# Attention outputs of two parity blocks transposed by one DMA, pad copies made for two blocks at once, and a new order of all jobs

## Chip, cores and metric

The kernel runs on one core of one Trainium2 chip. The metric is the device time of one execution in microseconds. The core has five engines with instruction queues of their own: TensorE (PE in the profile; PEld are its weight loads), VectorE (DVE), ScalarE (ACT), GpSimd (POOL) and SyncE (SP), which here only issues DMAs.

## The reference

One layer: an attention block, then a gated block with a product over the sequence, both behind a layer norm and with a residual.

```python
def _A_ref(x, wqkv, wo):                     # S = 2048, D = 448, H = 16 heads of 28
    W, dil = (8, 2)
    ...                                       # q, k, v = x @ wqkv
    off = jnp.arange(W) * dil                 # each position sees itself and 7 others, every second one back
    idx = pos[:, None] - off[None, :]
    ...
    attn = _softmax(logits, axis=-1)          # over the 8 positions, those before 0 masked out
    o = jnp.einsum('bhsw,bhswd->bhsd', attn, vg)
    return ... @ wo

def _B_ref(x, w_in, w_sp, b_sp, w_out):       # F = 1792, Fh = 896
    z = _gelu(jnp.einsum('bsd,df->bsf', x, w_in))
    z1 = z[..., :Fh]
    z2 = _layernorm(z[..., Fh:], axis=-1)
    g = jnp.einsum('ts,bsf->btf', w_sp, z2) + b_sp[None, :, None]
    return jnp.einsum('bsf,fd->bsd', z1 * g, w_out)

h = x + _A_ref(_layernorm(x), A_wqkv, A_wo)
out = h + _B_ref(_layernorm(h), B_w_in, B_w_sp, B_b_sp, B_w_out)
```

## The kernel before

All data stays on the chip in bf16; PSUM holds products in f32. The kernel is written as some 900 **jobs**, each a few instructions of one engine with the resources that they read and write. The constant `ORDER` (L33) is a list of job numbers: it is the order in which all jobs are issued to their engines' queues, found by a search ahead of time. Within an engine the list's order is the program's order; across engines, waits on semaphores follow from the resources. `BANKS` gives each use of PSUM its banks (of eight), `MODE` the way in which a product is split, `ON` the engine of a copy that several engines could make. Number 885 in `ORDER` (861 after the change) is a **warm** job: one matmul on constant data, put in where the plan has nothing for TensorE.

The names of jobs, with the tokens in 16 tiles `m` of 128:

- `x` loads, `st0`, `mv0`, `rs0`, `n0` (statistics, their sum, the root on POOL, the norm on VectorE) give a normalized tile in the ring `xn`. It has 448 columns and is padded to 512: copy `nd0` repeats its last 64 columns (L633), so that the fourth chunk of 64 inner rows lies on both halves of the partitions.
- `xT` turns a tile into columns: tiles 0 to 3 by TensorE with copies `xe`, tiles 4 to 15 by a transposing DMA on SP's queue.
- `qk2` to `qk5` (tiles of 256 or 512 tokens; `qk0`, `qk1` of 128) and `v` are the products with `wqkv`, copied out of PSUM by `qe` and `ve`.
- Attention runs in 17 **blocks** `b`. Blocks 0 to 15 come in pairs: an even one takes the even tokens of a stretch of 256, an odd one the odd ones; block 16 takes the rest. Per block: logits `lg` (two PSUM tickets, 28 inner rows each, four row groups at once), exponentials `ex` (ACT), mask `mk` (VectorE), output `o` (TensorE), `rc` and `om` (division, VectorE) into the ring `otm` of four slots, pad copy `od`, transposing DMA `oT` into `OTs`, and **column copy** `oc` from `OTs` into every second column of `OT` (L862), in two parts where the ring `OT` wraps (`oc8b`, `oc9b`).
- `y` projects two tiles with `wo` as soon as `OT` has their tokens (`COVER`), `h` adds the residual, `st1`, `mv1`, `rs1`, `n1`, pad copy `nd1` and transposing DMA `hT` (two tiles at once, L783) give the operand of the second block.
- `z2_m` and `z1_u` are the products with `w_in`, with `z2c`, `z2g`, `z1g` on ACT; `st2` to `n2` the second norm.
- `g` is the product with `w_sp`, `ua` and `um` the gate, `wo0` to `wo10` and `wp` the last product, `r` and `out` the result. `wlo` and `whi` are transposing loads of `w_sp`, `w_in0_0` and so on its weights.

A product of 448 inner rows has three full chunks and one of 64 rows. `MODE` 'FH' does the six full matmuls first and the two short ones, which run side by side on two row groups, second; 'HF' the other way; 'AB' cuts all into halves of 64 rows that run side by side, eight matmuls in part a and six in part b.

TensorE's order before, around the places that matter (part a and b of a product are two jobs):

```
... xT3 xT2 warm lg0_0 lg0_1 qk2_3a qk2_3b qk2_0a qk2_2a qk2_0b qk2_2b qk2_1a v2a qk2_1b v2b v0a lg2_0 lg1_0 v0b lg3_1 v4a v4b lg2_1 lg3_0 qk3_1a ...
... lg12_1 y4a lg12_0 lg13_1 y4b lg15_0 lg13_0 lg15_1 z2_1a o12 o10 v16a v16b lg16_0 z2_1b z2_2a ...
... y10a z1_0a y10b z1_0b z1_3a z1_6a z1_4a ...
```

SP's: `... x12 xT4 xT7 xT5 xT6 xT9 xT13 xT8 w_in0_1 xT10 xT11 xT12 xT14 oT0 oT1 xT15 w_in0_0 oT2 oT3 wlo5 ...`

Of the kernel before, what the change touches and what calls it, by code (L numbers as in the profile page):

```python
# [21 lines left out]
MODE = {'qk2_0': 'AB', 'qk2_1': 'AB', 'qk2_2': 'AB', 'qk2_3': 'FH', 'qk3_0': 'AB', 'qk3_1': 'AB', 'qk3_2': 'AB',  # L22
         'qk3_3': 'AB', 'qk4_0': 'AB', 'qk4_1': 'AB', 'qk4_2': 'AB', 'qk4_3': 'AB', 'qk5_0': 'AB', 'qk5_1': 'FH',
         'qk5_2': 'AB', 'qk5_3': 'FH', 'v0': 'AB', 'y0': 'AB', 'v2': 'AB', 'v4': 'FH', 'y2': 'AB', 'v6': 'AB', 'y4':
         'AB', 'v8': 'HF', 'y6': 'AB', 'v10': 'AB', 'y8': 'AB', 'v12': 'HF', 'y10': 'AB', 'v14': 'HF', 'y12': 'AB',
         'v16': 'FH', 'y14': 'AB', 'z2_0': 'AB', 'z2_1': 'AB', 'z2_2': 'AB', 'z2_3': 'HF', 'z2_4': 'AB', 'z2_5': 'AB',
         'z2_6': 'FH', 'z2_7': 'FH', 'z2_8': 'AB', 'z2_9': 'AB', 'z2_10': 'AB', 'z2_11': 'AB', 'z2_12': 'AB', 'z2_13':
         'AB', 'z2_14': 'AB', 'z2_15': 'AB', 'z1_0': 'AB', 'z1_1': 'AB', 'z1_2': 'FH', 'z1_3': 'HF', 'z1_4': 'FH',
         'z1_5': 'HF', 'z1_6': 'FH', 'z1_7': 'AB', 'z1_8': 'AB', 'z1_9': 'AB', 'z1_10': 'AB', 'z1_11': 'AB', 'z1_12':
         'AB', 'z1_13': 'AB', 'wo0': 'FF', 'wo2': 'FF', 'wo4': 'FF', 'wo6': 'FF', 'wo8': 'FF', 'wo10': 'FF'}  # L30
ORDER = [6, 26, 42, 27, 43, 29, 0, 885, 30, 885, 1, 31, 885, 885, 7, 885, 885, 28, 12, 885, 32, 885, 2, 52, 885, 134,
         885, 885, 5, 44, 33, 885, 885, 53, 3, 885, 34, 45, 54, 885, 135, 885, 4, 55, 46, 885, 885, 47, 16, 56, 885,
         885, 61, 35, 885, 9, 57, 48, 36, 885, 885, 59, 58, 885, 885, 11, 885, 37, 49, 62, 136, 885, 13, 885, 50, 145,  # L33
         38, 60, 51, 10, 63, 81, 146, 8, 137, 139, 82, 138, 39, 15, 140, 67, 64, 40, 17, 147, 83, 41, 148, 14, 84,
         141, 72, 85, 149, 70, 142, 150, 68, 73, 144, 71, 89, 65, 74, 69, 143, 885, 66, 94, 202, 75, 204, 160, 203,
         98, 76, 95, 161, 99, 77, 86, 205, 151, 90, 78, 87, 157, 96, 162, 152, 206, 158, 153, 154, 91, 159, 237, 79,
         97, 92, 155, 80, 113, 238, 156, 115, 199, 239, 114, 93, 88, 116, 117, 240, 100, 213, 119, 200, 241, 118, 253,
         120, 214, 201, 121, 262, 254, 104, 101, 105, 125, 263, 122, 242, 106, 264, 251, 110, 166, 123, 126, 102, 107,
         111, 252, 108, 127, 163, 243, 255, 167, 103, 164, 168, 256, 165, 207, 19, 257, 215, 244, 172, 109, 216, 258,
         169, 112, 217, 259, 173, 170, 208, 124, 174, 128, 209, 218, 129, 171, 245, 131, 219, 338, 132, 246, 339, 220,  # L40
         130, 247, 221, 210, 316, 248, 340, 178, 211, 317, 276, 305, 179, 222, 277, 181, 180, 306, 133, 212, 175, 265,
         18, 223, 278, 182, 266, 249, 176, 183, 279, 267, 260, 177, 280, 303, 184, 268, 224, 304, 697, 269, 185, 281,
         307, 186, 270, 21, 378, 250, 282, 693, 271, 283, 261, 314, 225, 272, 315, 698, 284, 379, 273, 226, 355, 380,
         300, 274, 318, 356, 341, 343, 301, 229, 344, 285, 227, 187, 342, 302, 190, 20, 228, 345, 692, 319, 308, 230,
         320, 275, 381, 321, 188, 23, 382, 231, 286, 22, 346, 309, 322, 189, 310, 191, 694, 287, 232, 192, 311, 347,
         233, 234, 392, 348, 288, 312, 235, 393, 193, 349, 289, 24, 353, 394, 194, 323, 354, 292, 290, 416, 417, 195,
         357, 395, 383, 293, 418, 196, 236, 384, 396, 313, 358, 324, 197, 350, 385, 454, 455, 198, 359, 25, 291, 360,
         397, 456, 294, 695, 421, 398, 325, 361, 399, 422, 352, 297, 419, 362, 295, 432, 351, 400, 326, 420, 296, 298,
         468, 327, 299, 433, 430, 423, 469, 470, 524, 471, 328, 424, 330, 431, 386, 699, 329, 425, 492, 387, 331, 426,
         493, 332, 495, 364, 388, 525, 363, 427, 494, 434, 534, 401, 526, 365, 472, 496, 535, 389, 366, 333, 536, 335,  # L50
         390, 334, 541, 457, 367, 336, 402, 542, 458, 337, 368, 435, 370, 543, 473, 436, 459, 371, 369, 497, 437, 372,
         460, 655, 474, 706, 475, 498, 438, 373, 476, 656, 461, 652, 544, 439, 499, 551, 653, 375, 374, 391, 657, 500,
         376, 545, 462, 428, 440, 654, 501, 552, 546, 403, 463, 553, 704, 547, 464, 558, 527, 465, 404, 377, 429, 502,
         554, 559, 528, 441, 537, 405, 649, 560, 466, 503, 538, 442, 529, 561, 650, 539, 707, 443, 658, 651, 667, 477,
         406, 444, 661, 446, 691, 445, 540, 696, 447, 408, 548, 659, 407, 555, 448, 504, 409, 549, 575, 660, 550, 556,
# [1079 lines left out]
```

## Time and profile before

| | us |
|---|---|
| median of 3 runs | 244.9 (244.74 to 245.12) |
| the profiled execution's own time | 247.0 |
| its span, first to last instruction | 245.3 |
| TensorE busy | 237.2 |
| VectorE busy | 147.6 |
| ACT busy | 91.1 |
| POOL busy | 42.5 |

The mean granted clock of TensorE was 0.993. In the profile a line like `L461` is a line of the kernel; L461 is the matmul of all products in `product`, L809 the logits, L833 the attention output, L987 and L1008 the product with `w_sp`, L1035 and L1056 the last one. `L504` is `move`, so every copy has that line and is told by its tiles. `psum<-wv,xhT` reads: writes psum, reads wv and xhT. "SPq" is a DMA's issue on SP's queue, "DMA a<-b" its transfer until it has landed. The timeline and the chain of waits give start, duration and instruction; in the timeline neighbours of one kind are merged ("x8").

### The profile page before, as it was taken

How to read it: one execution, taken by the hardware profiler on the slowest of the kernel's cores; microseconds unless marked ns; L12 is line 12 of the kernel's file. 1: busy time of each engine (PE TensorE's matmuls, PEld its weight loads, DVE VectorE, ACT ScalarE, POOL GpSimd, SP SyncE). 2: the span in 40 equal slices, each digit the busy share in tenths (PEclk: the TensorE clock that was granted, in tenths of full speed). 3: DMA queues.
4: the chain of work that ended last, by engine and by line, in shares of the span. 5: the costliest groups of instructions: out<-in, count | busy, mean ns of one | idle time of the engine just before them, and what ended most of it. 6: DMA issues, size and time to landing. Idle time of an engine off the chain costs nothing.

```text
span 245.3 us, 5632 instructions
## 1 busy us (share of the span) xinstructions
PE 237.2 (97%) x2422; PEld 122.3 (50%) x2422; DVE 147.6 (60%) x334; ACT 91.1 (37%) x109; POOL 42.5 (17%) x98
## 2 busy tenths in 40 slices
PE   7997999999999989999999999999999999999995
PEld 4763544554555534444555555555554444444453
DVE  5998685998999897899913030604217350060584
ACT  2485748968899956659711000000000000000000
POOL 6625022030533317052311000000000000000000
PEclk9997999999999999999999999999999999999999
DMA  6953527989688889957999700000000020000022
GB/s 175 294 157 70 129 61 110 189 174 186 128 107 112 88 146 225 253 59 134 166 178 181 141 3 0 3 0 3 0 3 0 0 92 24 0 3 0 3 90 97
DMA packets 66233, 23.20 MB, mean 95 GB/s; under 512 B 58656, under 2 KB 65952, under 8 KB 66208
## 3 DMA queue, kind: packets, MB, share of 16 engines
q1 hardware_dynamic: 66208, 22.83, 48.5%
q8 instruction: 19, 0.31, 0.5%
q14 instruction: 6, 0.05, 0.1%
HBM read 6.72 MB, written 1.84 MB: 35 GB/s over the span
## 4 chain that ended last, share of the span: by engine, by line
PE 80%; DMA 8%; DVE 7%; ACT 1%; SPq 1%; issue 1%; POOL 0%
PE psum L987 37%; PE psum L461 27%; PE psum L1035 7%; DMA hnT<-xn 4%; PE psum L1008 3%; PE psum L809 2%; PE psum L833 2%; PE psum L1056 2%; DMA wq<-in_A_wqkv_dram 2%; DVE st L620 2%; DMA xhT<-xn 2%; DVE E L824 1%; DVE xn L631 1%; DMA OTs<-otm 1%; DVE x_tm L774 1%; SPq L519 1%
## 5 line engine op out<-in xcount | busy, mean ns | idle before, releaser
L968 DVE TENSOR_TENSOR ub<-psum,bb 128x512 bf16<-128x512 f32 x28 | 18.1, 686 | 64.4 <-PE psum L987 64.4
L987 PE MATMUL psum<-wsp_hi,z2p 64*128 64x512 bf16 x384 | 42.2, 376 | 0.0
L818 ACT ACTIVATE E<-psum 128x960 bf16<-128x960 f32 (+2 forms) x34 | 31.5, 976 | 6.3 <-PE psum L809 6.3
L987 PEld LDWEIGHTS psum<-wsp_hi,z2p 64*128 64x128 bf16 x384 | 19.7, 94 | 21.9 <-DVE srg L1016 0.4
L987 PE MATMUL psum<-wsp_lb,z2p 64*128 64x512 bf16 x224 | 26.9, 376 | 0.0
L987 PE MATMUL psum<-wsp_la,z2p 64*128 64x512 bf16 x224 | 26.5, 376 | 0.0
L461 PE MATMUL psum<-w_in,hnT 64*128 64x448 bf16 (+1 forms) x206 | 24.6, 350 | 0.2 <-issue 0.2
L461 PE MATMUL psum<-hnT,w_in 64*128 64x512 bf16 (+1 forms) x166 | 23.7, 377 | 1.1 <-DMA hnT<-xn 0.9
L461 PE MATMUL psum<-xhT,wqk 64*128 64x512 bf16 (+3 forms) x206 | 24.4, 355 | 0.1
L898 DVE BATCH_NORM_STATS2 st<-z2p 128x6 f32<-128x448 bf16 x32 | 19.0, 610 | 8.0 <-ACT z2p L894 6.0
L824 DVE TENSOR_TENSOR E<-E,maskb 128x1920 bf16<-128x1920 bf16 (+2 forms) x17 | 19.8, 1183 | 2.9 <-ACT E L818 2.9
L620 DVE BATCH_NORM_STATS2 st<-x_tm 128x6 f32<-128x448 bf16 x32 | 18.8, 613 | 1.4 <-DMA x_tm<-in_A_x_dram 1.3
L987 PEld LDWEIGHTS psum<-wsp_lb,z2p 64*128 64x128 bf16 x224 | 12.8, 94 | 11.4
L987 PEld LDWEIGHTS psum<-wsp_la,z2p 64*128 64x128 bf16 x224 | 12.8, 94 | 11.4
L611 POOL TENSOR_TENSOR rs<-rs,negh 128x2 f32<-128x2 f32 (+2 forms) x23 | 17.4, 758 | 3.0 <-DVE rs L610 1.1
L936 ACT ACTIVATE z1p<-psum 128x1024 bf16<-128x1024 f32 x14 | 14.1, 1023 | 10.0 <-PE psum L461 10.0
L1035 PE MATMUL psum<-w_out,z1p 128*128 128x448 bf16 x84 | 16.4, 353 | 0.0
L461 PEld LDWEIGHTS psum<-w_in,hnT 64*128 64x128 bf16 (+1 forms) x206 | 10.9, 94 | 10.8 <-issue 1.0
L461 PE MATMUL psum<-wv,xhT 64*128 64x448 bf16 (+1 forms) x92 | 14.9, 367 | 1.4 <-DMA xhT<-xn 1.4
L504 ACT ACTIVATE qkT<-psum 128x1024 bf16<-128x1024 f32 (+1 forms) x17 | 13.3, 824 | 6.9 <-PE psum L461 4.2
L461 PEld LDWEIGHTS psum<-hnT,w_in 64*128 64x128 bf16 (+1 forms) x166 | 9.6, 95 | 12.4 <-DVE x_tm L774 1.4
L461 PEld LDWEIGHTS psum<-xhT,wqk 64*128 64x128 bf16 (+1 forms) x206 | 10.0, 95 | 9.8 <-issue 0.8
(68 smaller groups left out, 254.6 us busy)
## 6 DMA issues: line engine op xcount, KB each, us to landing
w_in<-in_B_w_in_dram SPq DMA_DIRECT2D x8, 224.0 KB, 3.7
out_dram<-srg SPq DMA_DIRECT2D x16, 112.0 KB, 1.7
x_tm<-in_A_x_dram SPq DMA_DIRECT2D x2, 448.0 KB, 5.2
w_out<-in_B_w_out_dram SPq DMA_DIRECT2D x1, 784.0 KB, 5.1
wq<-in_A_wqkv_dram SPq DMA_DIRECT2D x3, 224.0 KB, 4.5
x_tm<-in_A_x_dram SPq DMA_DIRECT2D x3, 224.0 KB, 3.4
bb<-in_B_b_sp_dram SPq DMA_DIRECT2D x1, 512.0 KB, 4.8
wv<-in_A_wqkv_dram SPq DMA_DIRECT2D x1, 336.0 KB, 4.8
```

Source lines behind the costliest of these rows:

```text
L461: ins = e.matmul(o, w, x, start=k not in seen, stop=last, **kw)
L504: j = pl.job(name, eng, key, [(lambda e: e.activation(o(), i(), AF.Copy) if eng == "act" else e.tensor_copy(o(), i()), list(reads), list(w ...
L611: power = (lambda e: e.tensor_tensor(R, A, negh[:, 0:1].to_broadcast([128, n]), ALU.pow), [rr, r_negh], r_rs[k][m:m + n])
L620: [(lambda e: e.bn_stats(st[:, m, :], src), [rsrc], [r_st[k][m]])], dve_t(D))
L818: return e.activation(o, i, AF.Exp, scale=SCALE)
L824: return e.tensor_tensor(a, a, maskb[:, mi:mi + 1, pad:pad + nq].to_broadcast([NK, NHEAD, nq]), ALU.mult)
L898: [(lambda e, m=m, k=k: e.bn_stats(st3[:, m, k, :], z2p[:, m, D * k:D * (k + 1)]), [r_z2[m]], [r_st[2][m]])], dve_t(D))
L936: return e.activation(o, i, AF.Gelu_apprx_tanh)
L968: [(lambda e: e.tensor_tensor(ub[:, s, :], psv(tk, k), bb[:, 512 * tc:512 * tc + 512], ALU.add), [r_bb], [r_ub[s]])], dve_t(512), use=[tk] ...
L987: ins = e.matmul(psv(tk, k), z2p[h, s, 128 * fc:128 * fc + 128], wsp(s, tc)[h], start=n == 0 and s == 0, stop=n == len(lots) - 1 and s == ...
L1008: ins = e.matmul(psv(tk), z2p[:, s, 128 * fc:128 * fc + 128], wsp(s, tc), start=(s == 0), stop=(s == NB - 1))
L1035: ins = e.matmul(psv(tk, k, D), z1p[h, fc, 128 * (m + k):128 * (m + k) + 128], w_out[h, fc, :], start=fc == 0 and (which == 0 or not half) ...
```

## The change

Three edits in the code, and new constants.

1. `project` no longer makes a pad copy `nd1` for each of two tiles; one copy, named `nd1_m` with the even m, does both, after the second norm.
2. For blocks 0 to 15 the pad copy `od` and the transposing DMA `oT` are made once for a pair, with the odd block's number: `od1`, `oT1`, `od3` and so on. The DMA takes two slots of `otm` (128 x 1024) into both halves of `OTs`. The column copies stay one per block and part; both blocks' copies follow the pair's DMA. Block 16 is as before.
3. `ORDER`, `BANKS`, `MODE` and `ON` are new. 24 jobs are gone.

```diff
             for i in range(2):
-                s = ln_norm(1, m + i, mv2, x_tm, r_h[m + i], kl, True)
+                s = ln_norm(1, m + i, mv2, x_tm, r_h[m + i], kl, False)
+            move("nd1_%d" % m, "pool", kl, lambda s=s: xn[:, s - 1:s + 1, D:512], lambda s=s: xn[:, s - 1:s + 1, 384:D], r_xn[s - 1:s + 1],
+                 r_xnd[s - 1:s + 1], {"pool": 0.5, "dve": 0.14})
...
-            move("od%d" % b, "pool", b + KEY["om"], lambda os=os, nq=nq: otm[0:nq, os, D:512], lambda os=os, nq=nq: otm[0:nq, os, 384:D],
-                 [r_otm[os]], [r_otd[os]], {"pool": 0.42, "dve": 0.1})
             t0 = k0 // step * step + step * pad
             if step == 1:
+                move("od%d" % b, "pool", b + KEY["om"], lambda os=os, nq=nq: otm[0:nq, os, D:512], lambda os=os, nq=nq: otm[0:nq, os, 384:D],
+                     [r_otm[os]], [r_otd[os]], {"pool": 0.42, "dve": 0.1})
                 dma_T("oT%d" % b, lambda o=t0 % OTR, n=nq: OT[:, :, o:o + n], lambda n=nq, os=os: otm[0:n, os, :],
                       [r_otm[os], r_otd[os]], [r_OT[t % OTR] for t in range(t0, t0 + nq)], b + KEY["oT"])
-            else:
-                dma_T("oT%d" % b, lambda b=b: OTs[:, b % 2], lambda os=os: otm[:, os, :], [r_otm[os], r_otd[os]], [r_OTs[b % 2]],
-                      b + KEY["oT"])
-                cut = min(nq, (OTR * (t0 // OTR + 1) - t0) // 2)
...
+            elif b % 2:
+                move("od%d" % b, "pool", b + KEY["om"], lambda os=os, nq=nq: otm[0:nq, os - 1:os + 1, D:512],
+                     lambda os=os, nq=nq: otm[0:nq, os - 1:os + 1, 384:D], r_otm[os - 1:os + 1], r_otd[os - 1:os + 1],
+                     {"pool": 0.5, "dve": 0.14})
+                load("oT%d" % b, lambda: OTs[:].rearrange("p m c t -> p (m c) t"), lambda os=os: otm[:, os - 1:os + 1, :],
+                     r_OTs, 1.3, (TLAT + 0.1, 1.0), key=b + KEY["oT"], transpose=True, reads=r_otm[os - 1:os + 1] + r_otd[os - 1:os + 1])
+                cut = min(nq, (OTR * (t0 // OTR + 1) - t0 // 2 * 2) // 2)
+                for par in range(2):
+                    for i, (a, z) in enumerate([(0, cut)] + ([(cut, nq)] if cut < nq else [])):
+                        o = (t0 + 2 * a) % OTR
+                        move("oc%d" % (b - 1 + par) + "b" * i, "pool", b + KEY["oT"],
...
```

What the constants come to, counted from the lists: warm jobs 29 before and 28 after. Engines of the copies that several can make: `ve` on VectorE four and two (`ve8` and `ve12` go to ACT); `oc` on POOL, ACT and VectorE 8, 7, 3 and 11, 4, 3; `nd` and `od` on POOL 24 and 16, on VectorE 21 and 13; weight copy `wp3` goes from VectorE to ACT; of the three `qe` on VectorE one is now `qe2_0`, of half the width. Jobs on SP: 113 and 105. Changes of TensorE's row grouping (full, halves, logits, transposes) from one job to the next: 73 before and 71 after, apart from those around the transposes on TensorE.

TensorE's order after, around the same places:

```
... qk0F2 xT2 xT3 qk0H qk1H warm warm qk2_2a qk2_3a qk2_3b qk2_2b lg0_0 lg0_1 qk2_0a qk2_1a qk2_0b qk2_1b v2a v0a lg3_0 lg2_0 v0b v2b v4a v4b lg3_1 o0 lg2_1 qk3_1a lg1_1 lg1_0 qk3_1b qk3_3a o3 o2 ...
... v14a lg10_1 qk5_3a qk5_3b v14b y4a lg12_0 lg15_1 y4b z2_1a z2_1b lg12_1 lg13_1 y6a lg13_0 y6b lg15_0 o10 o12 lg14_0 lg16_0 v16a v16b z2_2a ...
... z1_6b y10a z1_5b z2_5a y10b z1_3a z2_5b z1_3b z1_4a ...
```

SP's: `... x12 xT5 xT4 xT6 xT7 xT8 xT11 xT10 xT9 w_in0_0 w_in0_1 xT13 xT14 wlo5 oT1 xT12 xT15 oT3 wlo6 wlo1 ...`

VectorE's around the first transposes: `... n0_2 mv0_6 n0_3 mv0_5 st0_7 xe2_0 mv0_7 xe3_0 n0_5 st0_11 n0_4 mv0_11 st0_8 nd0_4 ...`, and around h4: `... mk9 mk11 h2 rc9 st1_2 rc11 om9 oc7 st1_3 om11 mk10 mv1_3 mv1_2 h4 n1_2 st1_4 st1_5 mv1_4 n1_3 mv1_5 mk12 h6 ...`

29 lines of the change are left out of this document (12 added, 17 removed), and 103 rows, old and new, of tables (BANKS, MODE, ORDER).

## The prediction

> **What bounds the kernel now.** I read the busy shares first, then the stages, then the waits of TensorE, then the timeline around them.
>
> ```profile
> PE 237.2 (97%) x2422; PEld 122.3 (50%) x2422; DVE 147.6 (60%) x334; ACT 91.1 (37%) x109; POOL 42.5 (17%) x98
> ```
>
> TensorE is busy 97% of the span. The matmuls to do stay the same, so the end moves only with the time in which TensorE waits or runs slowly. The stages tell where that is (from and to, length, then the busy time of PE, PEld, DVE, ACT and POOL with their instructions, the granted clock, the DMA share and GB/s):
>
> ```profile
> 0.00:20.00 20.00, 17.83 (x227) 12.53 (x229) 16.79 (x52) 10.88 (x18) 10.40 (x33) 1.00 0.71 200
> 20.00:21.70 1.70, 0.34 (x9) 0.20 (x8) 1.70 (x6) 1.70 (x3) 1.62 (x3) 1.00 0.47 71
> 21.70:25.40 3.70, 3.70 (x28) 1.35 (x30) 1.99 (x8) 1.24 (x3) 0.94 (x4) 0.54 0.37 75
> 25.40:66.20 40.80, 40.62 (x584) 20.32 (x580) 34.99 (x64) 30.80 (x36) 9.73 (x18) 1.00 0.74 137
> 66.20:68.10 1.90, 1.27 (x28) 0.74 (x28) 1.73 (x2) 1.90 (x3) 0.00 (x0) 1.00 0.83 179
> 68.10:88.40 20.30, 20.30 (x274) 10.81 (x274) 19.13 (x43) 19.05 (x24) 6.20 (x13) 1.00 0.85 108
> 88.40:89.50 1.10, 0.15 (x4) 0.08 (x2) 1.10 (x2) 0.95 (x1) 0.00 (x0) 1.00 0.97 97
> 89.50:123.60 34.10, 33.95 (x296) 16.49 (x298) 30.79 (x83) 22.61 (x26) 12.63 (x27) 1.00 0.91 168
> 123.60:245.30 121.70, 119.00 (x991) 59.77 (x985) 39.41 (x80) 1.94 (x2) 0.93 (x2) 1.00 0.19 40
> ```
>
> From 123.6 on, TensorE lacks only 2.7 us, which is the tail after the last matmul; a new order can gain nothing there. Before that it loses time in four places: the start, 20 to 25.4, 66.2 to 68.1 and 88.4 to 89.5. The last three have names:
>
> ```profile
> PE psum L461 <- DMA xhT<-xn: 1.4, 1, 1.4
> PE psum L461 <- DMA hnT<-xn: 0.9, 1, 0.9
> PE psum L809 <- DVE x_tm L774: 0.5, 1, 0.5
> ```
>
> ```profile
> 17.35 4.17 DMA xhT<-xn
> ```
>
> ```profile
> 57.22 0.42 PE L809 MATMUL psum<-qkT 28*128 28x120 bf16 x16
> 57.57 0.82 PE L461 MATMUL psum<-xhT,wqk 64*128 64x512 bf16 x6
> 58.23 1.59 PE L461 MATMUL psum<-wv,xhT 64*128 64x448 bf16 x8
> ```
>
> ```profile
> 21.66 2.62 PE L461 MATMUL psum<-wv,xhT 128*128 128x448 bf16 x8 [1.36 <-DMA xhT<-xn]
> ...
> 66.26 0.79 PE L809 MATMUL psum<-qkT 28*128 28x120 bf16 x16
> ...
> 67.52 0.39 PE L809 MATMUL psum<-qkT 28*128 28x120 bf16 x8 [0.47 <-DVE x_tm L774]
> ...
> 68.07 0.93 PE L461 MATMUL psum<-w_in,hnT 64*128 64x448 bf16 x8 [0.16 <-issue]
> ```
>
> The first is v4, which needs transpose xT5, third on SP's queue: issued at 17.35, landed 4.17 us later. TensorE stood still 1.36 us, and then the clock was near half (0.54) for 3.7 us. The eight matmuls of v4 took 2.62 us, those of v12 at full clock 1.59: 1.0 us, and some 0.2 us in the pieces behind it. The second is the logits around 66.3: 24 matmuls take 1.81 us to the next product (68.07 less 66.26), where 16 take 0.35 (57.57 less 57.22), so 24 want some 0.6; 1.2 us are lost, because h4 frees its PSUM bank late. The third is z1_3, which waited 0.9 us for transpose hT6. Together 1.4 + 1.2 + 1.2 + 0.9 = 4.7 us.
>
> **The change, part by part.** *Fewer transposes and copies.* Sixteen oT transposes become eight of double width, sixteen od copies eight, sixteen nd1 copies eight.
>
> ```profile
> L518 SPq DMA_TRANSPOSE OTs<-otm x16: 1190/1210/1676, 34.9 to 88.7; - x16
> L504 POOL COPY otm<-otm x9: 236/237/1257, 30.6 to 83.6; 120x64 bf16<-120x64 bf16 x8, 128x64 bf16<-128x64 bf16 x1
> L504 POOL COPY OT<-OTs x8: 617/744/1363, 37.4 to 93.2; 128x480 bf16<-128x480 bf16 x5, 128x512 bf16<-128x512 bf16 x2, 128x384 bf16<-128x384 bf16 x1
> ```
>
> ```profile
> L518 SPq DMA_TRANSPOSE hnT<-xn x8: 1231/1269/2364, 58.1 to 111.4; - x8
> ...
> DMA to landing us min/median/max: 3.1/3.8/5.2
> ```
>
> A transpose of double width already runs here, as hT: 1.27 us of SP's queue against 1.21 for one oT, so eight fewer free some 9 us of SP. POOL loses eight small copies net and takes eleven column copies (oc) where it had eight, 3 x 0.74 = 2.2 us more, roughly what the small ones free. None of this is TensorE's work: it lies beside it and is worth nothing until it makes an operand land earlier, which the next parts count. A copy of double width is not in the trace; I take 0.4 us on POOL, between 0.24 (one copy) and 0.48 (two), and it enters one chain below.
>
> ```profile
> 34.91 2.51 SPq L518 DMA_TRANSPOSE OTs<-otm  x2
> ```
>
> Pairing makes the even block wait for the odd one. Before, blocks 0 and 1 were transposed from 34.91, one behind the other. After, o1 comes some 1.5 us sooner, the one paired transpose goes out at about 33.5, lands by 36.5 (hT's median of 3.8 us less one for a queue with no other transpose ahead), and its two column copies on POOL end near 38. The projection y0 comes at about 39.6: before it stood at 42.60, and 2.6 us of idle and slow clock ahead of it are gone. So the wait for the odd block is covered by 1.6 us; without that cover it would cost what it is late. Where VectorE makes a column copy (oc2, oc4, oc7), it waits for the pair with its queue behind it: behind oc7 stand st1_3, om11 and mask mk10. By the work ahead oc7 comes near 59 and its transpose lands between 57.4 and 59.3, and o10, which needs mk10, is due near 67: nothing.
>
> *The order.* One warm matmul fewer (28 against 29) sits ahead of the first transposes, covered by the first normalization. TensorE changes its row grouping 71 times after and 73 before; I take both at nothing.
>
> **v4.** After the change SP issues xT5 and xT4 first and second. The last x copy of the first products ends at 13.23 in this trace:
>
> ```profile
> 12.63 0.60 DVE xhT L504
> ```
>
> ```profile
> L631 DVE TENSOR_SCALAR xn<-x_tm,mv,rs x32: 305/390/504, 5.5 to 110.8; 128x448 bf16<-128x448 bf16 x32
> ```
>
> ```profile
> 68.44 1.15 DVE L620 BATCH_NORM_STATS2 st<-x_tm 128x6 f32<-128x448 bf16 x2
> ```
>
> After, it ends near 12.9 (see the start, below), and VectorE goes on with norm n0_5 (0.39 us, its pad then on POOL), a statistic (0.58), norm n0_4 (0.39), another statistic and the pad of n0_4. So xT5 goes out near 13.9 and xT4 near 15.1.
>
> ```profile
> L518 SPq DMA_TRANSPOSE xhT<-xn x12: 1190/1264/2238, 14.7 to 37.5; - x12
> ...
> DMA to landing us min/median/max: 2.4/2.5/4.2
> ```
>
> From 15.1, 2.5 us gives 17.6 and the worst, 4.2, gives 19.3. The work ahead of v4 on TensorE ends near 20.1 as before. The wait goes, and with it the half clock: 1.4 + 1.2 us. The queue behind, xT6 and xT7, lands by 21 to 22, and their first reader qk3_1 comes at 22.8.
>
> One page speaks to the half clock: the Trainium skill, "TensorE: Matmul & The Clock Gate", section "Why this matters for your kernels", says the clock falls after gaps of TensorE over some 3 us. The trace disagrees: 1.36 us of idling was followed by 3.7 us at 0.54. By the page the slow stretch would not belong to this wait, and the change would win 1.2 us less; the row decides, and the page's case is a rival below.
>
> **The bank of y4 and z1_3.** After the change no logits tile reuses a bank within 1.1 us of TensorE work after its last user (before, lg15_1 followed y4a's bank by 0.2), and z1_3 comes later than hT6 can land. 1.2 + 0.9 us go.
>
> **New waits.** *Start:* the two x copies end 0.3 us earlier (one weight copy has gone to ACT, one norm less stands ahead), but two logits tiles with their switch, some 0.65 us, are not yet done then. Cost 0.4, between 0 and 0.8. *z2_2* needs hT2, and hT2 now starts from y4's end: h4, norm, two statistics, norm, one pair copy, transpose.
>
> ```profile
> L774 DVE TENSOR_TENSOR x_tm<-psum,x_tm x8: 1074/1092/1092, 47.0 to 105.2; 128x896 bf16<-128x896 f32 x8
> ```
>
> With the norm and the two statistics as above that is 1.09 + 0.39 + 1.15 + 0.39 + 0.4 + 3.8 = 7.2 us. Between y4 and z2_2 TensorE has z2_1 and y6, six logits tiles, o10, o12 and v16:
>
> ```profile
> 42.60 0.92 PE L461 MATMUL psum<-wo,OT 64*128 64x448 bf16 x8
> 43.36 0.81 PE L461 MATMUL psum<-xhT,wqk 64*128 64x512 bf16 x6
> 44.10 0.96 PE L833 MATMUL psum<-V,E 128*128 128x29 bf16 x32
> 45.00 0.93 PE L461 MATMUL psum<-wv,xhT 64*128 64x448 bf16 x8
> 45.86 0.39 PE L809 MATMUL psum<-qkT 28*128 28x120 bf16 x8
> 46.19 0.74 PE L461 MATMUL psum<-wo,OT 64*128 64x448 bf16 x6
> ...
> 69.75 1.02 PE L461 MATMUL psum<-wv,xhT 128*128 128x448 bf16 x4
> ```
>
> Start to start, the eight matmuls of a product's first part take 0.76 us, the six of its second 0.57 in proportion, so two products 2.66; the two o 0.90; v16 some 0.95 of its 1.02; four groups of logits, one or two tiles each, at 0.33 to 0.6 with the switch of row groups, 1.8: 6.3 us. TensorE waits 0.9 us; with the landing at its ends, 3.1 and 5.2, it is 0.2 and 2.3. *Three small ones,* 0.6 us together (0 to 1.2): qk3_1 behind v4's bank, o2 behind mask mk2, y8 behind the copies oc10 and oc11. *One late landing* that no row can place: the old order had two, 1.4 and 0.9 us; I take one of 0.9 (0 to 1.4).
>
> Sum: -4.7 + 0.4 + 0.9 + 0.6 + 0.9 = -1.9 us on a span of 245.3. The profiled execution took 247.0 with what lies around its span; the undisturbed runs have a median of 244.9, and the difference is carried over to that: **243.0 us**.
>
> **The rivals.** *Clean order:* hT2 lands at its best and nothing else is late: -4.7 + 0.4 + 0.2 + 0.6 = -3.5, 241.4. For it: SP has 9 us more room. Against: the landing's median.
>
> *Half clock at z2_2 (the other side):* hT2 at 5.2 makes TensorE wait 2.3 us instead of 0.9, longer than the 1.36 that took the clock down, so 1.2 us are lost behind it as well: 243.0 + 1.4 + 1.2 = 245.6, slower. It decides from about 1.9 us beyond the forecast, a landing some 0.7 us over the median where the clock does fall. For it: hT0 to hT6 all landed in the crowded stretch, and z2_2's place has no cover. Against: 0.95 us at 88.4 left the clock at 1.00.
>
> *VectorE takes over:* it is busy 30.79 of 34.10 us up to 123.6; if the operands of z2 and z1 come no earlier, TensorE gives back what it won before, and the end stays at about 244.9. Against: its queue grows shorter, by two value copies (ve8, ve12) that go to ACT, by eight small copies, and by a q copy of half the width.
>
> *The slow stretch belongs to another cause* and stays: 243.0 + 1.2 = 244.2.
>
> **How the numbers follow.** Forecast 0.45 (its own range 242.2 to 244.0), clean 0.20, half clock 0.20, VectorE 0.10, slow stretch 0.05. Runs of this kernel tell 0.2%, 0.5 us, from no change. Faster: 0.45 + 0.20 + 0.05 + part of VectorE's, 0.04 = 0.74; same 0.04; slower 0.22, the half clock and the rest. The range reaches from inside the clean case, 241.0, to the half-clock case, 245.6.
>
> **What would show it.** Right: no wait of TensorE on xhT, clock 1.00 between 20 and 26, nothing lost at the logits after y4, the sixteen OTs transposes eight at some 1.3 us of SP each, a wait on hnT near 70 of about 1 us. Wrong: the gate stage beginning no earlier than 123.6 less 1, half clock anywhere after 5 us, or a wait on OT before a projection, which would say that pairing costs more than its cover.

## The result and the profile after

The kernel after the change takes 243.29 us (median of 17 runs, 242.05 to 244.78), the kernel before, run beside it, 244.93 (17 runs): a ratio of 0.9933, with a 95% interval of 0.9913 to 0.9954. It is 1.6 us (0.7%) faster; 243.0 was predicted. The profiled execution of the changed kernel took 242.28 us with a span of 240.6, 1.0 us under its median, whereas the one of before (247.0) lay 2.1 us over. The two first traces therefore stand 4.7 us apart where the medians differ by 1.6, and several runs below serve to find out which part of the 4.7 is usual.

The line of busy shares of the changed kernel:

```profile
PE 235.2 (98%) x2441; PEld 116.0 (48%) x2441; DVE 142.5 (59%) x323; ACT 92.0 (38%) x109; POOL 41.9 (17%) x93
```

The same stretches as before the change, by stage (from and to, length, busy time of PE, PEld, DVE, ACT and POOL with their instructions, granted clock, DMA share, GB/s):

```profile
20.00:21.70 1.70, 1.70 (x18) 0.73 (x14) 1.70 (x5) 1.45 (x3) 0.07 (x1) 1.00 0.59 9
21.70:25.40 3.70, 3.70 (x64) 2.05 (x62) 3.70 (x9) 3.59 (x5) 0.24 (x1) 1.00 0.52 105
...
66.20:68.10 1.90, 1.88 (x50) 1.16 (x44) 1.59 (x2) 1.90 (x4) 1.82 (x3) 1.00 0.21 43
...
88.40:89.50 1.10, 1.10 (x14) 0.58 (x12) 1.10 (x3) 0.00 (x0) 0.29 (x1) 1.00 2.17 201
```

The three holes behind the start are filled (the first of them is two stretches here): TensorE is busy to within 0.02 us in each, 64 matmuls stand where 28 ran at half clock, and the clock is 1.00. What TensorE still waits for is in the view of its waits (us in total, times, the longest):

```profile
PE psum L1080 <- DVE warm L579: 1.9, 1, 1.9
PE psum L459 <- DVE xhT L502: 0.4, 1, 0.4
```

The first is the start itself, where the kernel before waited 1.4 us, the second the first products behind their x copies at 12.8. No wait on a transpose is left. Three of the moved steps (and v16, which stands ahead of the third), from TensorE's timeline (start, length, engine, line, operation):

```profile
39.01 0.92 PE L459 MATMUL psum<-wo,OT 64*128 64x448 bf16 x8
...
53.97 0.92 PE L459 MATMUL psum<-wo,OT 64*128 64x448 bf16 x8
...
69.11 1.03 PE L459 MATMUL psum<-wv,xhT 64*128 64x448 bf16 x4
69.98 1.78 PE L459 MATMUL psum<-w_in,hnT 128*128 128x448 bf16 x10
```

y0 comes at 39.01 (39.6 was forecast), y2 at 53.97, and z2_2 follows v16 at 69.98 without a wait. The paired transposes and the hT transposes, each from the view of its tile (shortest, median and longest ns of SP's queue, first and last start; under them issue to landing in us):

```profile
L516 SPq DMA_TRANSPOSE OTs<-otm x8: 1232/1303/2498, 33.3 to 86.1; - x8
...
DMA to landing us min/median/max: 3.0/3.8/5.3
```

```profile
L516 SPq DMA_TRANSPOSE hnT<-xn x8: 1232/1254/1382, 51.1 to 104.8; - x8
...
DMA to landing us min/median/max: 3.1/3.3/5.5
```

A pair costs SP 1.30 us where one block cost 1.21, as forecast, but takes 3.8 us to land where one took 2.9. hT lands in 3.3 us. The first trace of the kernel before had 3.8, but the second one, of the run before_again below, has 3.3 as well, so this is no gain of the change.

### The profile page after: what moved, and what is told of

The parts are those of the page before. It is cut to its first block, busy times and chain, and to the rows that moved or that the text cites. A ratio compares the mean times of both kernels' runs of the same rounds, so it can differ in the third digit from the quotient of the medians.

```text
span 240.6 us, 5652 instructions
## 1 busy us (share of the span) xinstructions
PE 235.2 (98%) x2441; PEld 116.0 (48%) x2441; DVE 142.5 (59%) x323; ACT 92.0 (38%) x109; POOL 41.9 (17%) x93
## 4 chain that ended last, share of the span: by engine, by line
PE 78%; DMA 9%; DVE 7%; SPq 2%; ACT 1%; POOL 1%; issue 0%; DVEq 0%
PE psum L990 37%; PE psum L459 26%; DMA OTs<-otm 7%; PE psum L1038 6%; PE psum L1011 3%; PE psum L1059 2%; DVE E L824 2%; DMA x_tm<-in_A_x_dram 2%; PE psum L833 2%; PE psum L809 2%; DVE st L618 2%; SPq L517 1%; SPq L516 1%; ACT E L818 1%; POOL OT L502 1%; DVE otm L844 1%
## 5 line engine op out<-in xcount | busy, mean ns | idle before, releaser
L990 PEld LDWEIGHTS psum<-wsp_hi,z2p 64*128 64x128 bf16 x384 | 18.6, 94 | 22.9 <-issue 0.4
L990 PE MATMUL psum<-wsp_lb,z2p 64*128 64x512 bf16 x224 | 26.3, 376 | 0.0
L459 PE MATMUL psum<-hnT,w_in 64*128 64x512 bf16 (+1 forms) x178 | 24.5, 377 | 0.0
L824 DVE TENSOR_TENSOR E<-E,maskb 128x1920 bf16<-128x1920 bf16 (+2 forms) x17 | 19.3, 1158 | 3.7 <-ACT E L818 3.5
L609 POOL TENSOR_TENSOR rs<-rs,negh 128x2 f32<-128x2 f32 (+2 forms) x23 | 18.4, 801 | 2.9 <-DVE rs L608 1.1
L990 PEld LDWEIGHTS psum<-wsp_lb,z2p 64*128 64x128 bf16 x224 | 10.9, 94 | 13.3
L990 PEld LDWEIGHTS psum<-wsp_la,z2p 64*128 64x128 bf16 x224 | 10.9, 94 | 13.2
L1038 PE MATMUL psum<-w_out,z1p 128*128 128x448 bf16 (+1 forms) x98 | 16.7, 352 | 0.0
L502 ACT ACTIVATE qkT<-psum 128x1024 bf16<-128x1024 f32 (+1 forms) x17 | 13.8, 852 | 5.5 <-PE psum L459 4.0
L1019 DVE TENSOR_TENSOR srg<-psum,x_tm 128x448 bf16<-128x448 f32 (+1 forms) x17 | 9.5, 592 | 9.7 <-PE psum L1038 7.7
```

The costliest lines, as they stand in the source:

```text
L459: ins = e.matmul(o, w, x, start=k not in seen, stop=last, **kw)
L502: j = pl.job(name, eng, key, [(lambda e: e.activation(o(), i(), AF.Copy) if eng == "act" else e.tensor_copy(o(), i()), list(reads), list(w ...
L609: power = (lambda e: e.tensor_tensor(R, A, negh[:, 0:1].to_broadcast([128, n]), ALU.pow), [rr, r_negh], r_rs[k][m:m + n])
L824: return e.tensor_tensor(a, a, maskb[:, mi:mi + 1, pad:pad + nq].to_broadcast([NK, NHEAD, nq]), ALU.mult)
L990: ins = e.matmul(psv(tk, k), z2p[h, s, 128 * fc:128 * fc + 128], wsp(s, tc)[h], start=n == 0 and s == 0, stop=n == len(lots) - 1 and s == ...
L1019: [(lambda e: e.tensor_tensor(srg[:, s, c0:c1], psv(tk, k, c1 - c0), x_tm[:, m, c0:c1], ALU.add), [r_x[m]], r_srg[2 * s + (c0 > 0):2 * s + ...
```

## The experiments

Each group of runs had its own runs of the kernel before beside it; their medians were 245.15 (35 runs), 245.15 (21), 244.84 (27) and 245.29 (9). The ratio is not the quotient of the two medians. Where the two differ most (before_waits_fixed 0.9925 against 0.9941, after_oT_undone 0.9980 against 1.0006), it is by 0.3% at most, and a difference as small as that is not told here. The kernels, by what they are:

| run | what it is | median, us | ratio to before | 95% interval |
|---|---|---|---|---|
| before_again | before, unchanged | 244.89 | 0.9992 | 0.9970 to 1.0013 |
| before_xt5_early | before, xT5 earlier | 243.99 | 0.9953 | 0.9930 to 0.9976 |
| before_waits_fixed | that, and two more moves | 243.71 | 0.9925 | 0.9894 to 0.9956 |
| before_xt5_last | before, xT5 later | 246.69 | 1.0076 | 1.0039 to 1.0112 |
| before_paired | old order, pairs | 248.00 | 1.0132 | 1.0094 to 1.0171 |
| before_paired_oc8 | that, oc8 on POOL | 246.02 | 1.0049 | 1.0016 to 1.0083 |
| after_pairs_undone | new order, no pairs | 245.17 | 1.0016 | 0.9987 to 1.0045 |
| after_oT_undone | new order, only nd1 paired | 245.29 | 0.9980 | 0.9951 to 1.0008 |
| after_nd1_undone | new order, only oT paired | 243.61 | 0.9936 | 0.9905 to 0.9966 |
| after_xt5_late | after, xT5 later | 244.97 | 0.9988 | 0.9961 to 1.0015 |
| after_again | after, unchanged | 243.37 | 0.9958 | 0.9929 to 0.9986 |
| after_third | after, unchanged | 243.43 | 0.9918 | 0.9885 to 0.9952 |

### Which of the four losses are usual: before_again

No edit.

> The kernel before, unchanged, for its spread and a second profile. The profiled execution took 247.0 us, 2.1 over the median of 244.9. Theory (the prediction): a usual execution has the wait of v4 on xhT, the late bank of y4 and the wait on hT6 too, so the new profile shows losses of TensorE of 4 us or more in the three places, and the granted clock is about 0.993 in most executions. Rival: the wait of v4 and the half clock behind it are an accident of that one execution; the clock is 1.00 in most, the span near 243.2, and the new profile shows at most 2.5 us lost in the three places.

Measured: 244.89 us; its profiled execution took 245.16, with a span of 243.4 and the clock at 1.00. TensorE's waits in it, and from its timeline the products of v4 and the logits behind y4:

```profile
PE psum L461 <- DMA xhT<-xn: 1.3, 1, 1.3
PE psum L461 <- DMA hnT<-xn: 1.1, 1, 1.1
PE psum L461 <- issue: 0.5, 3, 0.2
PE psum L809 <- DVE x_tm L774: 0.4, 1, 0.4
```

```profile
19.84 0.39 PE L809 MATMUL psum<-qkT 28*128 28x120 bf16 x8
21.51 1.59 PE L461 MATMUL psum<-wv,xhT 128*128 128x448 bf16 x8 [1.27 <-DMA xhT<-xn]
...
64.57 0.82 PE L809 MATMUL psum<-qkT 28*128 28x120 bf16 x16
...
66.43 0.93 PE L461 MATMUL psum<-w_in,hnT 64*128 64x448 bf16 x8 [0.21 <-issue]
```

The three waits are there again, with nearly the same sizes: v4 1.3, hT6 1.1, and the logits behind y4 with their late bank (1.86 us to the next product where 24 matmuls want some 0.6: 1.2 lost). What isn't there is the half clock: the eight matmuls behind a wait of 1.27 us take 1.59 us, not 2.62. So 3.6 of the 4.7 us that the prediction counted as gains are there without the half clock, and the 1.2 us of half clock are not. All 12 executions of this run have a mean clock of 0.999 or 1.00, where the theory had 0.993 in most.

### The wait of v4: before_xt5_early and after_xt5_late

```diff
 before_xt5_early, SP:
-xT4 xT7 xT5 xT6
+xT4 xT5 xT7 xT6      (and the pad copy nd0_5 right behind n0_5)
 after_xt5_late, SP:
-xT5 xT4 xT6 xT7
+xT4 xT6 xT5 xT7
```

> The kernel before with one thing moved: the pad copy of tile 5 goes ahead of mask mk0 on VectorE, and its transpose xT5 goes second on SP, ahead of xT7 and xT6. If the wait of v4 is in the usual execution: faster by 1.0 to 2.6 us (242.3 to 243.9). If it is an accident of the profiled one: within 0.5 us of before. In both cases no wait of v4 in the profile; qk3_1 may wait up to 0.5 us for xT6 in its place.

> The changed kernel with transpose xT5 third on SP, behind xT4 and xT6, as it was before. Theory (v4's wait was a main term): v4 waits again, 0.3 to 1.7 us, and where it waits over 1.3 us half clock follows: slower than the changed kernel by 0.5 to 2.6 us. Rival (v4's operand is hidden anyway): within 0.4 us of the changed kernel.

Measured: 243.99 us, ratio 0.9953, so 1.2 us less (0.6 to 1.7) for the first; 244.97 us, 1.7 more than the changed kernel's first median of 243.29, for the second. In before_xt5_early TensorE's waits no longer name xhT:

```profile
PE psum L463 <- DMA hnT<-xn: 1.0, 1, 1.0
...
PE psum L811 <- DVE x_tm L776: 0.4, 1, 0.4
```

v4 starts at 20.06 there instead of 21.51, and the later waits keep their size. This step of the prediction holds, at 1.2 us. In after_xt5_late v4 waited only 0.15 us, less than the 0.3 expected at least, but o0 behind it then waited 0.37 us for a value copy and began at 22.57 instead of 21.72: in the new order a late xT5 cost more than its own wait. The time is where the theory had it.

What made v4 late was more the landing of xT5 than its place on the queue. In seven traces with the old order the third transpose goes out between 17.06 and 17.55. In four of them (both of the kernel before, before_xt5_last and before_waits_fixed) it landed 4.1 to 4.2 us later, in the other three (before_xt5_early, before_paired and before_paired_oc8) 2.5 us later. With 2.5 us, xT5 would have landed at 19.85 in the first trace of the kernel before, ahead of the 20.30 at which v4 was due. The last section says what lay beside the late ones.

### Is the gain one of the order or of the pairs: after_pairs_undone and before_paired

```diff
 after_pairs_undone: after's ORDER, BANKS, MODE, ON; before's code; in each pair's place:
-od1 oT1 ... nd1_0 ...
+od0 od1 oT0 oT1 ... nd1_0 nd1_1 ...
 before_paired: before's ORDER, BANKS, MODE, ON; after's code; where the later of the two stood:
-... od0 ... oT0 ... od1 ... oT1 ... nd1_0 ... nd1_1 ...
+... od1 ... oT1 ... nd1_0 ...
```

> The order, banks and modes of the changed kernel with the code of before: each paired transpose, od and nd1 copy is two single ones at the same place of the order. Theory (the order is the gain, pairing lies beside TensorE's work): 243.3 us, within 0.5 of the changed kernel. Rival (pairing is the gain, by room on SP): 244.5 or more; then the profile shows TensorE waiting on OT or hnT, above all z2_2 behind hT2 and y6 behind oT9.

> The order, PSUM banks and row grouping of the kernel before, with the pairing alone: each paired pad copy, transpose and od copy stands where the later of its two single ones stood, and one column copy whose source would otherwise come after it moves behind the transpose. The 2x2 so far: the new order without pairing 245.2 against 245.15 (nothing), both together 243.3. Theory A, pairing is worth something only where the order counts on its earlier landings: in this order the projections were placed for single transposes, so pairing gives only the SP time in front of hT6 (two issues of 1.2 us fewer ahead of it: its wait of 1.0 us goes) and takes nothing elsewhere: 244.2 us (243.7 to 244.7). Theory B, pairing is worth its 1.9 us by itself wherever it stands: 243.2. Theory C, the even block's wait for the odd one costs more here than it frees, since no job was moved to allow for it: over 245.5, with a wait of TensorE on OT ahead of a projection.

Two limits of these edits: the single transposes stand where the pair stood, so the even one goes out no earlier than it would in the pair; and small copies change their engine with the edit (in after_pairs_undone six more are on VectorE; in before_paired nd1_2, for one, goes from VectorE to POOL).

Measured: the new order without pairs takes 245.17 us, and the pairs in the old order 248.00. So the order alone gains nothing that can be told (0.9987 to 1.0045), the pairs alone cost 2.9 us, and both together gain 1.6. The profiled execution of after_pairs_undone took 246.37 us, 1.2 over its median. TensorE's waits in it have two new lines of over 1 us, and its timeline shows where they are:

```profile
PE psum L464 <- ACT OT L507: 1.6, 1, 1.6
PE psum L464 <- DVE OT L507: 1.3, 1, 1.3
```

```profile
54.99 0.93 PE L464 MATMUL psum<-wo,OT 64*128 64x448 bf16 x8 [1.25 <-DVE OT L507]
...
96.39 0.93 PE L464 MATMUL psum<-wo,OT 64*128 64x448 bf16 x8 [1.57 <-ACT OT L507]
```

They are y2 and y14: projections whose column copies come late because two transposes stand on SP where the new order counts on one. SP's queue and VectorE's timeline in front of y2:

```profile
46.69 4.47 SPq L521 DMA_TRANSPOSE OTs<-otm  x2
```

```profile
53.47 0.62 DVE L847 TENSOR_TENSOR otm<-psum,rcp 120x448 bf16<-120x448 f32 x1 [1.42 <-DMA OTs<-otm]
54.01 0.92 DVE L507 COPY OT<-OTs 128x480 bf16<-128x480 bf16 x1
```

oT4 and oT5 hold the queue for 4.47 us, of which one alone takes 3.11, VectorE stands still 1.42 us for them, and y2 comes at 54.99 instead of 53.97. In before_paired the loss is at another place, on ACT. Its timeline, and TensorE's beside it:

```profile
62.07 0.96 ACT L821 ACTIVATE E<-psum 128x960 bf16<-128x960 f32 x1
65.11 0.31 ACT L505 ACTIVATE OT<-OTs 128x96 bf16<-128x96 bf16 x1 [2.08 <-DMA OTs<-otm]
65.30 3.53 ACT L821 ACTIVATE E<-psum 128x960 bf16<-128x960 f32 x4
```

```profile
66.30 0.42 PE L812 MATMUL psum<-qkT 28*128 28x120 bf16 x16 [2.15 <-ACT E L821]
67.16 0.93 PE L462 MATMUL psum<-w_in,hnT 64*128 64x448 bf16 x8 [0.44 <-ACT E L821]
```

The small column copy oc8 (128 x 96, 0.31 us) now waits for the pair oT9, which holds block 9, too, and ACT stands still 2.08 us with four exponentials behind it. These free the PSUM banks of the logits, so TensorE waits 2.15 and 0.44 us. That is the mechanism that the prediction's working feared for VectorE's oc7 and found covered; in the old order it decides, on ACT. Theory C had the size, over 245.5, but not the place: the wait is on E and not on OT. The price has a second part, since behind the 2.15 us the clock was 0.50 from 68.5 to 71.9, and all six executions have a mean clock of 0.993 or less. And it is reckoned against a kernel that waits at v4; in this trace v4 did not wait, though the order up to there is the same.

### The price of that queue: before_paired_oc8

```diff
 before_paired, ON:
-'oc8': 'act'
+(oc8 on POOL)
```

> before_paired (248.0 us) with one thing changed: the column copy oc8, which waits for the paired transpose oT9, runs on POOL instead of ACT. In before_paired ACT stood 2.1 us in front of it with the exponentials ex12_0, ex13_1 and ex15_0 behind it, and TensorE then waited 2.2 us for the PSUM bank that ex12_0 frees. Theory A, the pairing's price in the old order is this queue on ACT: the wait of 2.2 us on E goes, and with it the most of the 2.9 us: 245.2 to 246.0 us. Theory B, the later half of each pair holds back the whole chain from the projections to z2, and ACT only showed it: 247.3 to 248.2, with a wait of 2 us on x_tm, hnT or OT in its place.

Measured: 246.02 us, 2.0 less than before_paired and 1.2 more than the kernel before. TensorE's waits on E of 2.2 and 0.4 us are gone; in their place stand

```profile
PE psum L462 <- DMA hnT<-xn: 1.1, 1, 1.1
...
PE psum L462 <- POOL OT L505: 0.6, 1, 0.6
```

The first is at 70.27, z2_2 behind hT2: oc8b and oc8 now hold POOL's queue until oT9 lands, and the pad copy nd1_2 that hT2 needs stands behind them (in the kernel before it was on VectorE). So theory A holds for two thirds, and the rest went where theory B said: a copy that waits for the second half of a pair holds up what is queued behind it, on POOL as on ACT. Part of the 2.0 us is the half clock, which 2 of 12 executions show here and all six of before_paired did.

### Which pairs carry it: after_oT_undone and after_nd1_undone

```diff
 after's constants; after_oT_undone: nd1 paired, otherwise
-od1 oT1
+od0 od1 oT0 oT1
 after_nd1_undone: od and oT paired, otherwise
-nd1_0
+nd1_0 nd1_1
```

> The changed kernel with its order, banks and row grouping, the pad copies of the normalized rows (nd1) left paired, but the attention outputs transposed one block at a time (two od copies and two oT transposes in each pair's place). With both undone it took 245.2, with both paired 243.3. Theory A, the 1.9 us come from SP and the transposes: 245.0 us (244.5 to 245.5), with the same two waits of TensorE on column copies into OT as with both undone (1.3 to 1.6 us each). Theory B, they come from the POOL copies ahead of hT: 243.5, and no such wait.

> The changed kernel with its order, banks and row grouping, and its paired transposes of the attention outputs, but the pad copies of the normalized rows (nd1) single again, two in each pair's place. Theory A (the gain is SP's and the transposes'): 243.4 us (243.1 to 243.9), no wait on OT; the second copy puts each hT some 0.3 us later, seen at most as a short wait on hnT. Theory B (the gain is POOL's): 245.0.

Measured: 245.29 us with the transposes single, 243.61 with the pad copies single. In the first, TensorE's waits have the column copies again:

```profile
PE psum L463 <- ACT OT L506: 2.1, 2, 1.7
...
PE psum L463 <- POOL OT L506: 0.6, 1, 0.6
```

Its timeline shows them at y2, y10 and y14:

```profile
55.00 0.93 PE L463 MATMUL psum<-wo,OT 64*128 64x448 bf16 x8 [0.63 <-POOL OT L506]
...
87.92 1.30 PE L463 MATMUL psum<-wo,OT 128*128 128x448 bf16 x6 [1.70 <-ACT OT L506]
...
95.70 1.69 PE L463 MATMUL psum<-wo,OT 64*128 64x448 bf16 x16 [0.44 <-ACT OT L506]
```

They are 2.8 us together, as much as the two at y2 and y14 with both undone, but spread otherwise. In after_nd1_undone there is no such line. The two kernels, run side by side, lie 1.7 us apart by their medians and 1.1 by their ratios. The gain of pairing is that of the paired transposes; pairing the pad copies of the normalized rows is worth no more than these runs can tell.

### Do the waits add up: before_waits_fixed

```diff
 before_xt5_early, and on TensorE:
-lg15_1 z2_1a
+z2_1a lg15_1
 on SP:
-wlo12 hT6
+hT6 wlo12
```

> The kernel before with the three named waits of TensorE taken away by moves alone and nothing paired: xT5 and its normalization first (as in the run before_xt5_early), the logits tile lg15_1 behind z2_1's first part so that h4's PSUM bank is free, and hT6 ahead of the transposed load of one weight half on SP. Theory A, the terms of the prediction are independent and add: v4's wait 1.0 (measured in the first group of runs), the bank 0.7 to 1.2, hT6 0.9 to 1.0, together 2.6 to 3.2 off 245.15, 242.0 to 242.5 us, so the new order and the pairing would not be needed for the gain. Theory B, the places lie in series behind VectorE, and each wait taken away comes back at the next operand: 243.6 to 244.0, with new TensorE waits on hnT, xhT or x_tm.

Measured: 243.71 us, ratio 0.9925: 1.8 us less than before (1.1 to 2.6), where theory A said 2.6 to 3.2. The wait of z1_3 on hT6 is gone without a successor. That of the logits is not: TensorE's timeline has in the same place

```profile
65.55 0.93 PE L463 MATMUL psum<-w_in,hnT 64*128 64x448 bf16 x8 [0.64 <-ACT E L820]
```

z2_1, moved ahead, waits for a bank that an exponential on ACT frees. The waits of v4 and hT6, 2.4 us by the trace of before_again, lie within the interval; of the 1.2 us at the bank at least half came back, and whether the rest was gained these runs can't tell. The medians alone differ by 1.4 us. Three moved steps in the old order, with no pairing, thus come as near to the gain as can be told from the whole change (0.9925 against 0.9933).

### What a usual execution of the changed kernel waits for: after_again and after_third

No edits.

> The changed kernel unchanged, for a second profile and its time beside the others of this group. Its profiled execution was 1.0 us under its median of 243.3. Theory A, the few waits of that execution are what the order leaves and the rest is spread: median 243.3 (242.9 to 243.7), span 240.6 to 242.6, clock 1.00, no wait on hnT or xhT over 0.5 us. Theory B, the order hangs on a lucky landing of one transpose (hT2 in 3.15 us): a wait on hnT near 70 of 0.5 us or more.

> The changed kernel unchanged, for a third profile: its two profiled executions so far, 242.28 and 241.96 us, lay 1.0 and 1.4 us under the medians of their groups (243.29 and 243.37). If this one takes 243 us or more, its trace shows what the usual execution has beyond those two. Theory A, a landing near 50 to 75 us comes later there (hT2, or one of the paired oT transposes): a wait of 0.5 us or more on hnT, OT or the column copies. Theory B, the start: the loads of x land later and everything behind moves with them, TensorE's waits as before. If it takes 242.5 or less, what the usual execution has beyond it stays open.

Measured: 243.37 and 243.43 us. The profiled execution of after_again was again a short one (241.96 us, span 240.2), but that of after_third took 244.15 with a span of 242.4, 0.7 over its median, and its trace has what the others lack. From its waits of TensorE, its timeline of TensorE, and SP's:

```profile
PE psum L459 <- POOL OT L502: 1.5, 1, 1.5
...
PE psum L459 <- DMA hnT<-xn: 0.3, 1, 0.3
```

```profile
94.18 1.69 PE L459 MATMUL psum<-wo,OT 64*128 64x448 bf16 x16 [1.54 <-POOL OT L502]
```

```profile
82.64 0.58 SPq L517 DMA_DIRECT2D bb<-in_B_b_sp_dram  x1
83.27 1.16 SPq L516 DMA_TRANSPOSE wsp_la<-in_B_w_sp_dram  x1
84.55 1.25 SPq L516 DMA_TRANSPOSE OT<-otm  x1
85.85 4.34 SPq L516 DMA_TRANSPOSE OTs<-otm  x1
```

The paired transpose oT15, behind the load of bb (512 KB) and the last of its kind, held the queue for 4.34 us and landed 7.5 us after its start; y14 waited 1.54 us for its copy on POOL. In the first trace of the changed kernel the same DMA was quicker, and POOL and TensorE had

```profile
86.08 2.50 SPq L516 DMA_TRANSPOSE OTs<-otm  x1
```

```profile
91.47 0.72 POOL L502 COPY OT<-OTs 128x480 bf16<-128x480 bf16 x1 [2.61 <-DMA OTs<-otm]
```

```profile
92.33 1.68 PE L459 MATMUL psum<-wo,OT 64*128 64x448 bf16 x16
```

The copy ended at 92.19 and y14 began at 92.33: a cover of 0.14 us. So theory A of the last expectation holds in kind but not in place: the late landing is that of oT15, at 93.4 us and not between 50 and 75. None of the three profiled executions lay at the median of 243.3 to 243.4, so how much of this wait a usual one has stays open. The load of bb alone does not explain it: in after_again oT15 stood behind it, too, and took 1.31 us. An order with oT15 ahead of the load of bb was not tried.

### The half clock: before_xt5_last

```diff
 before, SP:
-xT4 xT7 xT5 xT6
+xT4 xT7 xT6 xT5
```

> The kernel before with xT5 moved one place back on SP, behind xT6, so that v4's wait on TensorE grows from 1.3 us to between 2.5 and 4. In the first profiled execution of the kernel before, a wait of 1.36 us was followed by 3.7 us at a granted clock of 0.54; in the second one of 1.3 us was followed by full clock. Theory A, a gap takes the clock down once it is longer than about 3 us (the Trainium skill, TensorE: Matmul & The Clock Gate, Why this matters for your kernels): with a gap over 3 us the clock falls in every execution, and the time is some 1.2 us beyond the added wait: 248 to 249 us. Theory B, the half clock of the first execution came from something else in it than the gap: the clock stays at 1.00 and the time is 246.3 to 247.7, the added wait alone.

Measured: 246.69 us, ratio 1.0076. The gap did not reach the 2.5 us that were meant: xT5 landed sooner behind its issue, and v4 waited 1.52 us. The stretches around it (columns as above):

```profile
20.23:21.75 1.52, 0.01 (x1) 0.04 (x2) 1.45 (x4) 1.52 (x2) 1.44 (x3) 1.00 0.21 16
21.75:24.35 2.60, 2.60 (x12) 0.83 (x16) 1.73 (x7) 0.03 (x1) 0.61 (x3) 0.56 0.27 54
24.35:25.40 1.05, 1.05 (x20) 0.56 (x22) 0.00 (x0) 1.02 (x2) 0.00 (x0) 0.50 0.61 124
25.40:30.00 4.60, 4.60 (x74) 2.45 (x70) 3.44 (x4) 3.05 (x4) 0.00 (x0) 0.99 0.61 135
```

There it is again: full clock up to the gap, 0.56 and 0.50 for 3.65 us behind it, then full clock. A stretch of 3.7 us at 0.54 lowers the mean over a span of 245 us by 0.46 x 3.7 / 245 = 0.007, so an execution that had one shows a mean granted clock of 0.993. Counted that way, 16 of 104 executions of the kernel before in these groups had it (the wait at v4 is 1.36 us in the trace that has the stretch, 1.27 in the one that has not), 4 of 8 of before_xt5_last (1.5 us), all 6 of before_paired (2.15 us; two of them have 0.986 and 0.985, room for two stretches), and none of the 12 of before_xt5_early and the 7 of before_waits_fixed, where v4 doesn't wait. In the first group of runs the executions of before with it have a median of 246.93 us and the others 245.05. Neither theory of the expectation holds: the clock does fall behind this gap, at 1.5 us already, but not in every execution. A gap over 3 us, the condition of theory A, did not come about.

## Why the prediction was right, and where it was not

The time was right and so was the direction, and most of the reasons held. But the half clock among the gains and the new waits among the costs were both counted too high and cancelled, so it is in part luck that 243.0 came within 0.3 us of the median; and the part on the pairing was wrong.

**v4.** The wait of 1.4 us was rightly read and rightly given up by the change; taking it away alone, in the old order, gained 1.2. xT5 went out at 13.57 (13.9 was forecast) and landed 3.8 us later, xT4 at 15.5 (15.1) and landed 2.5 us later, at 18.0, inside the 17.6 to 19.3 given.

**The half clock.** It does belong to that wait, as the trace had it: of the rival "the slow stretch belongs to another cause" little is left, since 16 of 104 executions of the kernel before have the stretch and none of the 19 without the wait, where that rate would give three. Two things were wrong with the term. One was the carrying over: the sum was made on a profiled execution that had this stretch, and its 1.2 us were then taken off a median that mostly lacks it. The row that could have warned was the distance itself: 247.0 against 244.9. The other was the size: the prediction read it from v4 and the pieces behind it, but the clock was 0.50 for 3.41 us, which is 1.7 us of TensorE's work, and the executions with the stretch are 1.9 us longer (246.93 against 245.05).

**The bank behind y4, and hT6.** Both waits are usual (1.2 us and 1.1 in before_again), and both are gone after the change.

**The new waits.** Start 0.4: the second x copy ended at 12.77 against the 12.9 forecast, and the 0.4 of the first products is in the waits. z2_2 0.9: it was 0 in two traces and 0.28 in the third; hT2 landed 3.15 us after its issue, at its best and not at its median of 3.8, as the clean rival had it. Three small ones, 0.6: none of them is in any of the three traces with more than 0.2. One late landing that no row could place, 0.9 with bounds of 0 and 1.4: 0, 0 and 1.54 us in the three traces, at oT15 and y14. Of these four terms, 2.8 us together, the three traces show 0.4 to 2.2.

**The sum** for an execution without the half clock is thus -3.6 (1.3, 1.2 and 1.1) and +0.4 to 2.2, together -3.2 to -1.4; the medians say -1.6. The gains were counted 1.1 too high (4.7 against 3.6) and the costs 0.6 to 2.4 too high, and the two cancelled.

**The pairing.** This is the step that failed. The prediction put it that the saved time of SP and POOL "lies beside it and is worth nothing until it makes an operand land earlier", and then counted no operand that does. There are such operands, the column copies ahead of y2, y10 and y14: with single transposes at the pair's place the new order waits there for 2.8 us in each of two traces, and its gain of 1.6 us is gone. An order made for single transposes was not tried. The prediction compared the pairs with the old order, in which the projections had room; it didn't ask what the new order's projections, y0 at 39.0 instead of 42.6 and all behind it, would meet if SP still made sixteen transposes. Nor are the pairs good in themselves: in the old order they cost 2.9 us, of which 2.0 go with one small copy on ACT that waits for the odd block with exponentials behind it, the half clock behind that wait included. The prediction named that mechanism and checked VectorE's three copies for it; in the traces of the new order it was right that those three cost nothing.

**VectorE takes over** did not come: its busy time up to 120 us is 103.26 us after, against 108.39 up to 122.9 in before_again. Of TensorE's waits on it only those at the start are longer (1.9 us against 1.4, and 0.4 at the first products).

**The signs.** No wait on xhT from a DMA, full clock in all three traces, no loss at the logits, eight transposes at 1.3 us: all as said. One of the 37 executions of the changed kernel (245.61 us) does have a mean clock of 0.993; no trace shows where. The last product ahead of the gate stage began at 120.0 in the first trace and 121.9 in the third, against 123.3 in the first one before, so this sign of being wrong stayed away. A wait on hnT near 70 of about 1 us: not there. A wait on OT before a projection, the sign that pairing costs more than its cover: not in the first trace, but in the third, at y14.

## What to carry to other kernels

A merged transfer and the order around it are one change: try each alone before crediting either, for here the order gains nothing, the merging loses 2.9 us, and both gain 1.6. Try the plain repair beside them, too: three moved steps in the old order, with nothing merged, came to the same time as far as these runs can tell. Merging makes the first half wait for the second, so look at each engine whose queue holds a small copy of the merged result, and at what stands behind that copy. And before a sum made on one profiled execution is carried to the median, ask which of its terms made that execution differ from the median.

## What the runs showed of the hardware

The clock falls to about half behind gaps of TensorE well below 3 us, and not each time: behind some 1.3 us at v4 in 15% of the executions, behind 1.5 in 4 of 8, behind 2.15 in 6 of 6 (gaps as the traces show them, executions counted by their mean clock). In the three traces that have the slow stretch it is 3.41 us at 0.50, and it begins not with the first matmul behind the gap but 0.30, 0.33 and 2.20 us later (before, before_xt5_last, before_paired). The Trainium skill, "TensorE: Matmul & The Clock Gate", section "Why this matters for your kernels", warns of gaps over some 3 us; these runs disagree. The length of the gap isn't all: the 12 executions of after_oT_undone had none, though its trace has a wait of 1.7 us near 88, between products. What at v4 makes the difference stays open. before_paired_oc8 and after_pairs_undone had 2 and 1 of 12 executions with a mean clock of 0.993, in places that no trace shows.

One and the same transpose can hold SP's queue for very different times: oT15 took 1.31, 2.50 and 4.34 us in the three executions of the changed kernel. The long ones came where the records show an instruction fetch (some 16 KB, on the queue q8) while it was in flight. From the view of DMA traffic of after_third, 88.0 to 90.2:

```profile
q8 instruction: 1, 0.02, 2.7%
```

In after_again that fetch came within 82.6 to 85.8 instead, where another transpose, a load of a weight half, took 2.64 us. In after_nd1_undone and after_xt5_late oT15 had a fetch beside it, too, and took 2.43 and 3.30 us.

The other traces say the same. All 14 together hold 426 transposes between tiles on the chip that start before 110 us and have on SP's queue either no such fetch beside them or one for more than 0.5 us: the 359 without one took 1.25 us in the median, nine of them over 1.45; the 67 with one took 2.11, and 58 of them over 1.45. And it fits the wait of v4, as far as seven traces go: in the four where the third transpose landed after 4.1 to 4.2 us, a fetch began 1.91 to 1.98 us behind its issue; in the three where it landed after 2.5 us, the fetch began 2.26 us behind it or later. No run moved the fetch alone, so this is a strong coincidence and not a cause shown.
